# A written order for VectorE's first steps, one query load on another queue, and block sums moved later

## The chip, the cores and the metric

The program runs on one core of one Trainium2 chip. The metric is the device time of one execution in microseconds (us), as the median of several runs. A core has five engines with queues of their own: TensorE (PE, matmuls), VectorE (DVE), ScalarE (ACT), GpSimd (POOL) and SyncE (SP, which here only issues DMAs). An engine takes its instructions strictly in the order of its queue; an instruction that waits holds up everything behind it on the same engine.

## The reference

An attention with a local window and block summaries, then two gated layers over its output, in fp32:

```python
# q, k, v: (2, 8, 768, 64); block 32, window 16, nb = 24
k_sum = k.reshape(B, H, nb, block, D).max(axis=3)
v_sum = v.reshape(B, H, nb, block, D).mean(axis=3)
scores_l = where(|pos_q - pos_k| < window, scale * q @ k^T, -1e9)
scores_s = scale * q @ k_sum^T + log(block)
a = softmax over concat([scores_l, scores_s])      # + 1e-9 in the denominator
attn = a @ concat([v, v_sum])
x = attn as (1536 tokens, 512)
h = x @ w_in;  x = (h * sigmoid(1.702 * h)) @ w_out          # d_ff 2048
y = (sigmoid(x @ w_gate) * (x @ w_val)) @ w_out2             # d_ff 1536
```

The layers' weights arrive as 64-bit floats.

## The kernel before

**Units.** The attention is cut into 24 units: 2 batches, 3 groups of 256 tokens (`g`), 4 pairs of heads (`hp`). Unit u is (batch, g, hp) with hp fastest, so units 0 to 11 are batch 0. For each unit the kernel runs, in this order:

- `w_copy` (POOL): scales the keys of the group and the block maxima of the keys (`kmax`, from `prep_k` on VectorE, one per batch and pair of heads) into a tile `kx`, of which there are two.
- `b_pe` (TensorE): scores `ps_s` from `kx` and the unit's queries (`load_q`), on top of a mask.
- `b_max` (VectorE): the row maximum `nm`. `b_exp` (ScalarE): four exponentials with row sums. `n_inv` (VectorE): adds epsilon to the sums and takes the reciprocal `rr`. `n_mul` (POOL): multiplies.
- `c_pe` (TensorE): transposes; `c_copy` copies them out (ScalarE for the first ten units, then VectorE).
- `d_pe` (TensorE): products with a window `vwin`, whose rows are the values of the group (`load_v`) and the block sums of the values (`put_v`, a DMA from the tile `vsum`). For the first group of batch 0 the sums come by separate matmuls straight from `vsum`. `d_hi` and `d_lo` write the result as two parts, `xH` and `xL`.

**Block sums of the values.** `sum_load` loads one pair of heads, transposed, through SP (batch 1 through two buffers, so the third load waits for the first sum). `sum_v` reduces it on VectorE into `vm`, and `sum_lay` lays the four out with matmuls on TensorE (`ps_v`) and scales them on ScalarE into `vsum`. `put_v` then copies `vsum` into a window.

**The loop.** One Python loop runs t from -1 to 26. In iteration t the parts stand as `ORDER` says: `w_copy` of unit t+1, scores, maximum and exponentials of unit t, reciprocal of t-1, multiplication of t-2, transposes and products of t-3. The products of unit 0 come one iteration later, behind `sum_lay(0)` at t = 4. The loads, sums and weight steps of the iteration stand behind them. `pull` runs the next step of the weight decode (`load`, lines 106 to 167: `da`, `db`, hi and lo parts of a weight, on VectorE and ScalarE; a step may issue the next weight DMA through `fetch`). `next(fill)` adds matmuls of the first layer for tokens already done (`filler`; ps_h into the hidden, ps_o out of it); the steps for the first 512 tokens begin at t = 10.

**Who sets the order.** SP's queue keeps the order of the source (`manual_schedule`). On the other engines a planner at compile time places the instructions by its own estimate of time, with the source's order as priority. `behind(a, b)` forbids it to place a ahead of b; it adds no wait on the chip. Before the change it holds for POOL (`in_turn`, to unit 8), for TensorE's scores among themselves, for `sum_lay(0)` behind the newest scores, and for batch 0's sums behind the newest maximum. VectorE's other steps have no written order.

**After the attention** the two layers run on TensorE from a written order of products; it is not touched.

Of the kernel before, what the change touches and what calls it, by code (L numbers as in the profile page):

```python
# [24 lines left out]
EPS = 1e-9  # L25
# [4 lines left out]
def attention_moe_moe2_kernel(ctx: ExitStack, tc: tile.TileContext, ins: dict, out: bass.AP):  # L30
# [544 lines left out]
    IN_TURN = 8  # L575
    coming = (x for n, key in enumerate(wanted) for x in load(*key, n < 2))
# [13 lines left out]
    with tc.manual_schedule(engines={mybir.EngineType.SP}), ExitStack() as es:  # L590
# [15 lines left out]
        SH = S + 2 * HALO  # L606

# [44 lines left out]
        def sum_v(b, hp):  # L652
# [7 lines left out]
            if b == 0:  # L660
                behind(ins, topped[-1])

        def sum_lay(b):
            r = vpart.pop(b)
            ps = ps_a.tile([W0, H * D], F32, tag="x", name="ps_v", bufs=2)
            for hp in range(HP):
                ins = nc.tensor.matmul(ps[:, hp * P:(hp + 1) * P], lhsT=r[:, hp], rhs=ident, start=True, stop=True)
                if b == 0:
                    behind(ins, scored[-1])
            nc.scalar.activation(vsum[b][0:W0], ps, AF.Copy, scale=1.0 / BLK)  # L670

        def prep_k(b, hp):
# [3 lines left out]
            nc.vector.tensor_reduce(out=ks[:, 0:NB], in_=own, axis=AX.X, op=ALU.max)  # L676
# [12 lines left out]

        live, scored, topped, spread = {}, [], [], []  # L690

        def behind(a, b):

            tc.add_manual_dep(
                a.ins, b.ins.name,
                mybir.DependencyInfo(mybir.DependencyClass.NoSync, mybir.DependencyReason.DATA), reason="order",
            )

        def in_turn(ins, u):

            if u <= IN_TURN:
                if spread:
                    behind(ins, spread[-1])
                spread.append(ins)
# [13 lines left out]
        def b_max(u):  # L718
            nm = sp.tile([P, G], F32, tag="nm", name="nm")
            topped.append(nc.vector.tensor_reduce(out=nm, in_=live["s", u], axis=AX.X, op=ALU.max, negate=True))  # L720
# [12 lines left out]
        def n_inv(u):  # L733
            rs = sp.tile([P, G], F32, tag="rs", name="rs")
            nc.vector.tensor_scalar(out=rs, in0=live.pop(("sum", u)), scalar1=EPS, scalar2=None, op0=ALU.add)
            rr = sp.tile([P, G], F32, tag="rr", name="rr")
            nc.vector.reciprocal(out=rr, in_=rs)
# [69 lines left out]
        for i in range(HP):  # L807
            load_q(i, nc.scalar)
            load_k(0, i)
        for i in range(HP):  # L810
            sum_load(0, i)
        load_v(0, 0)
        load_q(4, nc.sync)
        load_q(5, nc.sync)
        load_v(0, 1)
        load_q(6, nc.sync)
        load_q(7, nc.sync)
        fetch()
# [37 lines left out]
        for t in range(-1, NU + LD):  # L856
# [3 lines left out]
            if u < NU and units[u][1] == 0:  # L860
                prep_k(units[u][0], units[u][2])
            for part, lag in ORDER:
# [3 lines left out]
                if 0 <= t - lag < NU and not (late and t == LD):  # L866
                    part(t - lag)
                if (part, t) == (b_pe, LD + 1):
# [4 lines left out]
            if 0 <= t < HP:  # L873
                sum_v(0, t)
# [4 lines left out]
            if t in (7, 8, 9, 10):  # L879
                sum_load(1, t - 7)  # L880
            if t in (8, 9, 10, 11):
                sum_v(1, t - 8)
# [164 lines left out]
```

## Time and profile before

| | us |
|---|---|
| runs | 620.97, 621.0, 622.27 (median 621.0) |
| profiled execution, its own time | 620.25 |
| span, first to last instruction | 618.5 |
| TensorE busy in the span | 602.6 (97%) |
| VectorE | 465.8 (75%) |
| ScalarE | 307.6 (50%) |
| POOL | 213.5 (35%) |

The span of the profiled execution is 1.75 us shorter than its time; what lies around it is launch and end. The profile has several views. Busy time by stretch shows which engine is full where. An engine's order of time gives each instruction with its start, its length and, in brackets, the idle time before it and what ended that. The list of waits sums these up. The chain that ended last is followed back from the last instruction. DMAs are listed with the time from issue to landing. In all of them `out<-in` names the tiles and L12 is a line of the kernel. Two records of one matmul (x8 for four) stand where an fp32 matmul runs in two passes. Tile names carry no unit number: units are counted from the first.

### The profile page before, as it was taken

To read this page: it belongs to the slowest core of one execution; us is meant where nothing else is said; L and a number is where in the kernel's file an instruction comes from. 1 tells how busy PE (TensorE), PEld (TensorE's weight loads), DVE (VectorE), ACT (ScalarE), POOL (GpSimd) and SP (SyncE) were. 2 spreads that over 40 slices of the span, in tenths; PEclk is the share of its full clock that TensorE was granted. 3 is DMA by queue.
4 is the path that set the end of the run, shared out by engine and by line. 5 is a ranking of instruction groups with operands and counts; after the bars stand their busy time and mean duration, and the time that the engine had idled before them with its cause. 6 is when DMAs were issued, how large, how long until landed. Compare 5 with 4: busy or idle time off the path is not lost.

```text
span 618.5 us, 8840 instructions
## 1 busy us (share of the span) xinstructions
PE 602.6 (97%) x3356; PEld 500.6 (81%) x3360; DVE 465.8 (75%) x684; ACT 307.6 (50%) x614; POOL 213.5 (35%) x168
## 2 busy tenths in 40 slices
PE   7898999999999999999999999999999999999997
PEld 3775778788878888888888898888898898898896
DVE  7499665389998778796769889576968768877434
ACT  5587757656443354434445566644335435444230
POOL 6897686323372413232241232021121121131030
PEclk9799999999999999999999999999999999999999
DMA  9999733035121103040102013310312222100014
GB/s 325 333 305 340 239 86 69 2 103 170 68 69 68 40 30 137 1 137 3 67 0 69 1 29 110 134 69 27 110 69 69 68 69 70 68 1 1 0 48 156
DMA packets 25162, 58.10 MB, mean 94 GB/s; under 512 B 1569, under 2 KB 1825, under 8 KB 25121
## 3 DMA queue, kind: packets, MB, share of 16 engines
q1 hardware_dynamic: 24400, 56.24, 27.8%
q10 hardware_dynamic: 720, 1.31, 0.6%
q8 instruction: 26, 0.43, 0.3%
q14 instruction: 16, 0.12, 0.1%
HBM read 53.08 MB, written 3.15 MB: 91 GB/s over the span
## 4 chain that ended last, share of the span: by engine, by line
PE 80%; issue 5%; DVE 5%; DMA 4%; ACT 3%; POOL 3%; SPq 0%; ACTq 0%; POOLq 0%; DVEq 0%
PE ps_o L474 33%; PE ps_y L178 15%; PE ps_x L178 10%; PE ps_v L178 10%; PE ps_h L474 4%; PE ps_h L178 4%; DMA q<-in_q 2%; POOL gl L494 2%; PE ps_x L767 2%; PE ps_s L714 2%; DMA raw<-in_moe_w_out 1%; PE ps_p L748 1%; ACT e L728 1%; DVE db L123 1%; DVE sg L485 1%
## 5 line engine op out<-in xcount | busy, mean ns | idle before, releaser
L494 POOL TENSOR_TENSOR gl<-sg,gh 128x512 fp32r<-128x512 f32 x84 | 126.0, 1506 | 361.7 <-ACT gh L493 259.8
L557 DVE TENSOR_TENSOR acc<-ps_o,acc 128x512 f32<-128x512 f32 x143 | 96.0, 683 | 46.7 <-PE ps_o L474 46.6
L493 ACT CAST gh<-sg 128x512 fp32r<-128x512 f32 x84 | 51.5, 620 | 49.4 <-DVE sg L485 39.9
L474 PE MATMUL ps_o<-gl,w_1H 128*128 128x512 f32 x192 | 75.5, 394 | 0.5 <-POOL gl L494 0.5
L474 PE MATMUL ps_o<-gh,w_1H 128*128 128x512 f32 x192 | 74.7, 390 | 0.0
L474 PE MATMUL ps_o<-gh,w_1L 128*128 128x512 f32 x192 | 72.5, 397 | 1.0 <-ACT acc L553 0.9
L474 PE MATMUL ps_o<-w_2L,gh 128*128 128x512 f32 (+1 forms) x146 | 56.7, 388 | 0.0
L474 PE MATMUL ps_o<-w_2H,gh 128*128 128x512 f32 (+1 forms) x146 | 56.3, 387 | 0.0
L474 PE MATMUL ps_o<-w_2H,gl 128*128 128x512 f32 (+1 forms) x146 | 56.2, 389 | 0.1
L137 DVE SCALAR_TENSOR_TENSOR da<-da,db 128x1024 uint32<-128x1024 uint32 x34 | 47.7, 1402 | 5.6 <-ACT da L131 4.8
L131 ACT ACTIVATE da<-da 128x1024 f32<-128x1024 f32 x34 | 36.1, 1061 | 23.5 <-DVE da L123 23.4
L474 PEld LDWEIGHTS ps_o<-gh,w_1L 128*128 128x128 f32 x192 | 36.0, 188 | 9.0 <-ACT acc L553 1.4
L474 PEld LDWEIGHTS ps_o<-gl,w_1H 128*128 128x128 f32 x192 | 36.1, 188 | 8.6 <-POOL gl L494 1.5
L474 PEld LDWEIGHTS ps_o<-gh,w_1H 128*128 128x128 f32 x192 | 36.1, 188 | 7.2
L728 ACT ACTIVATE e<-ps_s,nm 128x128 f32<-128x128 f32 x96 | 34.2, 377 | 8.1 <-DVE nm L720 5.9
L474 PE MATMUL ps_h<-xL,w_0H 128*128 128x512 f32 x96 | 37.9, 395 | 0.2 <-DVE xL L788 0.2
L474 PE MATMUL ps_h<-xH,w_0L 128*128 128x512 f32 x96 | 37.8, 402 | 0.3 <-ACT xH L785 0.3
L474 PE MATMUL ps_h<-xH,w_0H 128*128 128x512 f32 x96 | 37.5, 390 | 0.0
L687 POOL TENSOR_SCALAR kx<-k 128x384 f32<-128x384 f32 x24 | 32.0, 1334 | 14.0 <-PE ps_s L714 8.7
L485 DVE TENSOR_TENSOR sg<-ps_h,sg 128x512 f32<-128x512 f32 x32 | 21.8, 682 | 14.2 <-ACT sg L501 12.1
L474 PEld LDWEIGHTS ps_o<-w_2H,gh 128*128 128x128 f32 x146 | 27.4, 188 | 5.7
L714 PE MATMUL ps_s<-kx,q 128*128 128x128 f32 x192 | 27.7, 287 | 4.3 <-DMA q<-in_q 2.1
(242 smaller groups left out, 1502.8 us busy)
## 6 DMA issues: line engine op xcount, KB each, us to landing
raw<-in_moe_w_out SPq DMA_DIRECT2D x13, 1024.0 KB, 4.9
raw<-in_moe_w_in SPq DMA_DIRECT2D x8, 1024.0 KB, 7.3
raw<-in_moe_w_gate SPq DMA_DIRECT2D x6, 1024.0 KB, 5.1
raw<-in_moe_w_val SPq DMA_DIRECT2D x6, 1024.0 KB, 5.1
q<-in_q SPq DMA_DIRECT2D x20, 256.0 KB, 9.7
vwin<-in_v SPq DMA_DIRECT2D x6, 768.0 KB, 9.4
k<-in_k SPq DMA_DIRECT2D x8, 400.0 KB, 6.8
out<-acc SPq DMA_DIRECT2D x11, 256.0 KB, 2.0
```

The source lines that it names most:

```text
L131: nc.scalar.activation(af, af, AF.Prelu, scale=REBIAS, alpha=-2.0 ** 32)
L137: nc.vector.scalar_tensor_tensor(out=a, in0=a, scalar=3, in1=b, op0=ALU.logical_shift_left, op1=ALU.bitwise_or)
L178: nc.tensor.matmul(ps, lhsT=a[x][:, kk, :], rhs=b[y][:, kk, :], start=start and i == 0, stop=i == n - 1, skip_group_check=True,)
L474: nc.tensor.matmul(ps, lhsT=a, rhs=b, start=i == 0, stop=i == n - 1)
L485: nc.vector.tensor_tensor(out=sg, in0=val, in1=sg, op=ALU.mult)
L493: nc.scalar.copy(gh, sg)
L494: nc.gpsimd.tensor_tensor(out=gl, in0=sg, in1=gh, op=ALU.subtract)
L557: nc.vector.tensor_tensor(out=a[:, m, :], in0=ps, in1=a[:, m, :], op=ALU.add)
L687: in_turn(nc.gpsimd.tensor_scalar(out=to, in0=x, scalar1=scale, scalar2=None, op0=ALU.mult), u)
L714: ins = nc.tensor.matmul(ps[:, j, :], lhsT=t[:, j, :], rhs=kt[:, j, :], start=False, stop=j == G - 1)
L728: nc.scalar.activation(e[:, j, :], s[:, j, :], AF.Exp, bias=nm[:, j:j + 1], accum_out=sm[:, j:j + 1])
L767: nc.tensor.matmul(ps[64 * e:64 * e + 64, j, :], lhsT=x[:, h * D:(h + 1) * D], rhs=y[:, j, 64 * e:64 * e + 64], start=n == 0, stop=n == le ...
```

## The change

Four parts, all in the attention and its loop.

1. A chain `next_up` on VectorE: each instruction handed to it is placed behind the one before. In it stand batch 0's key maxima and value sums, the row maxima and the two reciprocal steps of units 0 to 4, the row maxima from unit 10 on and batch 1's value sums. `prep_k` moves from the head of the iteration to behind `b_max`; batch 0's sums move to the places below.
2. The queries of unit 4 (`load_q(HP, nc.scalar)`) are issued by ScalarE's queue, ahead of the sums' loads in the source; those of unit 5 go ahead of the first value window, those of units 6 and 7 ahead of the second.
3. Batch 1's value-sum loads move from t = 7 to 10 to t = 8 to 11, the sums from t = 8 to 11 to t = 10 to 13, `sum_lay(1)` from t = 11 to t = 13.
4. `sum_lay(1)` is now behind the newest scores too, and the copy `put_v(1, 0)` follows it at t = 13 instead of standing at t = 11.

```diff
+    FIRST_UNITS = 5
...
+        def next_up(ins, when=True):
+            if when:
+                if turn:
+                    behind(ins, turn[-1])
+                turn.append(ins)
...            # sum_v
-            if b == 0:
-                behind(ins, topped[-1])
+            next_up(ins)
...            # sum_lay
-                if b == 0:
-                    behind(ins, scored[-1])
+                behind(ins, scored[-1])
...            # prep_k
-            nc.vector.tensor_reduce(out=ks[:, 0:NB], in_=own, axis=AX.X, op=ALU.max)
+            ins = nc.vector.tensor_reduce(out=ks[:, 0:NB], in_=own, axis=AX.X, op=ALU.max)
+            if b == 0:
+                next_up(ins)
...            # b_max
-            topped.append(nc.vector.tensor_reduce(out=nm, in_=live["s", u], axis=AX.X, op=ALU.max, negate=True))
+            ins = nc.vector.tensor_reduce(out=nm, in_=live["s", u], axis=AX.X, op=ALU.max, negate=True)
+            next_up(ins, u < FIRST_UNITS or u >= NU // 2 - 2)
...            # n_inv, both of its instructions
+            next_up(ins, u < FIRST_UNITS)
...            # loads ahead of the loop
+        load_q(HP, nc.scalar)
         for i in range(HP):
             sum_load(0, i)
+        load_q(5, nc.sync)
         load_v(0, 0)
-        load_q(4, nc.sync)
-        load_q(5, nc.sync)
-        load_v(0, 1)
         load_q(6, nc.sync)
         load_q(7, nc.sync)
+        load_v(0, 1)
...            # the loop
-            if u < NU and units[u][1] == 0:
-                prep_k(units[u][0], units[u][2])
             for part, lag in ORDER:
...
+                if part is b_max and u < NU and units[u][1] == 0:
+                    prep_k(units[u][0], units[u][2])
+                if part is b_max and t in (2, 3):
+                    sum_v(0, t - 1)
...
-            if 0 <= t < HP:
-                sum_v(0, t)
+            if t in (1, 3):
+                sum_v(0, 0 if t == 1 else 3)
...
-            if t in (7, 8, 9, 10):
-                sum_load(1, t - 7)
             if t in (8, 9, 10, 11):
-                sum_v(1, t - 8)
-            if t == 11:
+                sum_load(1, t - 8)
+            if t in (10, 11, 12, 13):
+                sum_v(1, t - 10)
+            if t == 13:
                 sum_lay(1)
+                put_v(1, 0)
...            # at t = 7, 11, 15, 19
                 load_v(c // NG, c % NG)
-                put_v(c // NG, c % NG)
+                if c != NG:
+                    put_v(c // NG, c % NG)
```

## Rows read from the trace of the kernel before

**Rows 1.** Stretch: length; busy PE, PEld, DVE, ACT, POOL; clock; DMA share; GB/s

```profile
0.00:15.40 15.40, 10.85 (x51) 5.86 (x51) 11.42 (x35) 8.21 (x27) 10.36 (x18) 1.00 0.91 325
15.40:22.30 6.90, 4.49 (x20) 3.61 (x21) 2.38 (x7) 2.58 (x10) 6.90 (x9) 0.51 1.06 300
25.00:50.00 25.00, 23.69 (x285) 18.84 (x284) 23.23 (x46) 21.86 (x81) 20.83 (x17) 1.00 1.05 329
50.00:70.00 20.00, 16.88 (x125) 12.37 (x127) 18.75 (x29) 16.44 (x43) 13.80 (x11) 1.00 0.80 252
100.00:600.00 500.00, 499.50 (x2538) 421.31 (x2538) 384.31 (x519) 238.62 (x391) 136.03 (x88) 1.00 0.17 59
```

**Rows 2.** TensorE in order of time: start, us, what [idle before <-releaser]

```profile
14.85 0.66 PE L748 MATMUL ps_p<-ident,e 128*128 128x128 f32 x4 [1.75 <-POOL e L742]
17.58 2.04 PE L714 MATMUL ps_s<-kx,q 128*128 128x128 f32 x8 [2.08 <-DMA q<-in_q]
19.56 1.92 PE L667 MATMUL ps_v<-ident,vm 128*32 128x128 f32 x8
...
23.88 1.16 PE L714 MATMUL ps_s<-kx,q 128*128 128x128 f32 x8
```

**Rows 3.** The chain that ended last, in order: start, us, what

```profile
8.63 8.82 DMA q<-in_q
...
61.94 1.51 ACT e L728 x8
...
114.01 5.49 PE ps_h L474 x24
```

**Rows 4.** VectorE in order of time, 8 to 16 us

```profile
8.80 0.68 DVE L720 TENSOR_REDUCE nm<-ps_s 128x4 f32<-128x512 f32 x1
...
11.05 0.94 DVE L656 TENSOR_REDUCE vm<-vt 128x24 f32<-128x768 f32 x1
...
13.44 0.17 DVE L737 RECIPROCAL rr<-rs 128x4 f32<-128x4 f32 x1
...
15.10 0.94 DVE L656 TENSOR_REDUCE vm<-vt_early 128x24 f32<-128x768 f32 x1
```

**Rows 5.** POOL in order of time, 13 to 26 us

```profile
13.76 1.04 POOL L742 TENSOR_TENSOR e<-e,rr 128x512 f32<-128x512 f32 x1 [2.43 <-DVE rs L735]
...
16.39 1.04 POOL L742 TENSOR_TENSOR e<-e,rr 128x512 f32<-128x512 f32 x1
...
25.20 1.17 POOL L687 TENSOR_SCALAR kx<-k 128x384 f32<-128x384 f32 x1 [2.50 <-PE ps_s L714]
```

**Rows 6.** DMAs issued in 6.9-8, 36.1-36.5, 38.1-39, 52.5-52.8: count, KB, us to landing

```profile
vt_early<-in_vt SPq DMA_DIRECT2D x1, 384.0 KB, 6.8
...
raw<-in_moe_w_out SPq DMA_DIRECT2D x1, 1024.0 KB, 13.3
...
k<-in_k SPq DMA_DIRECT2D x1, 400.0 KB, 13.2
...
vt<-in_vt SPq DMA_DIRECT2D x1, 384.0 KB, 6.3
```

**Rows 7.** VectorE in order of time, 42 to 75 us

```profile
42.30 0.94 DVE L656 TENSOR_REDUCE vm<-vt 128x24 f32<-128x768 f32 x1
...
46.02 0.68 DVE L720 TENSOR_REDUCE nm<-ps_s 128x4 f32<-128x512 f32 x1
...
49.67 0.68 DVE L123 TENSOR_SCALAR db<-raw 128x1024 uint32<-128x1024 uint32 x1
...
74.42 1.26 DVE L123 TENSOR_SCALAR db<-raw 128x1024 uint32<-128x1024 uint32 x1 [2.33 <-DMA raw<-in_moe_w_out]
```

**Rows 8.** TensorE's waits, 50 to 70 us: us in total, times, longest

```profile
PE ps_v L667 <- DVE vm L656: 1.2, 3, 0.7
...
PE ps_s L714 <- POOL kx L687: 0.8, 1, 0.8
```

**Rows 9.** SP's waits 40 to 80 us, and its order of time

```profile
SPq L635 <- ACT xH L785: 10.7, 1, 10.7
...
64.88 0.61 SPq L635 DMA_DIRECT2D vwin<-vs  x1
```

More of the change, by code (lines that the diff above doesn't have):

```diff
@@ L606, in attention_moe_moe2_kernel, with behind, in_turn @@
         SH = S + 2 * HALO
+        live, scored, spread, turn = {}, [], [], []
+        def behind(a, b):
+            tc.add_manual_dep(
+                a.ins, b.ins.name,
+                mybir.DependencyInfo(mybir.DependencyClass.NoSync, mybir.DependencyReason.DATA), reason="order",
+            )
+        def in_turn(ins, u):
+            if u <= IN_TURN:
+                if spread:
+                    behind(ins, spread[-1])
+                spread.append(ins)
+        def next_up(ins, when=True):
[3 more added lines that the diff above has]
+                turn.append(ins)
         def load_k(b, hp):
@@ L688, in w_copy @@
             kx[u] = t
[L690 to L704, printed above, removed]
         def b_pe(u):
@@ L734, in n_inv @@
             rs = sp.tile([P, G], F32, tag="rs", name="rs")
-            nc.vector.tensor_scalar(out=rs, in0=live.pop(("sum", u)), scalar1=EPS, scalar2=None, op0=ALU.add)
+            ins = nc.vector.tensor_scalar(out=rs, in0=live.pop(("sum", u)), scalar1=EPS, scalar2=None, op0=ALU.add)
+            next_up(ins, u < FIRST_UNITS)
             rr = sp.tile([P, G], F32, tag="rr", name="rr")
-            nc.vector.reciprocal(out=rr, in_=rs)
+            ins = nc.vector.reciprocal(out=rr, in_=rs)
+            next_up(ins, u < FIRST_UNITS)
             live["rr", u] = rr
```

## The prediction

> **What bounds the kernel now.** I read the busy time of each engine by stretch first [rows 1]. From 100 to 600 us TensorE is busy 499.5 of 500 us at the full clock, so what is won or lost ahead of 100 us comes out at the end one for one, unless another engine becomes later than TensorE there. What is left to win lies ahead: 4.55 us idle to 15.4, 2.41 us to 22.3, 1.31 us from 25 to 50, 3.12 us from 50 to 70. In the second stretch the granted clock is 0.51, the lower of the two levels (1.2 GHz), so its work takes twice as long as well.
>
> Second, TensorE's own order of time says what it stood before [rows 2]. Ahead of unit 0's transposes (14.85) it waits 1.75 us for POOL, after them 2.08 us for unit 4's queries. Unit 4's scores then take 2.04 us where unit 5's, at the full clock, take 1.16, and the block sums laid out behind them take 1.92, about 1.0 at the full clock (half). Only then come the first products with the values and unit 5's scores at 23.88. Third, the chain of waits gives the reason for the longer wait [rows 3]: the queries of unit 4 are issued at 8.63 and are 8.82 us under way, to 17.45. Fourth, VectorE's and POOL's order [rows 4, 5]: VectorE reduces block sums (0.94 each) between unit 0's maximum at 8.80 and its reciprocal at 13.44. POOL, which takes each unit's kx and each multiplication in a fixed order, stands idle 2.43 us for that reciprocal, and later 2.50 us for unit 5's scores. Last, the transfers. From 15 to 50 us the DMA share is 1.05 to 1.06 [rows 1]: there, data land in the order of their bytes, however soon the engines are done.
>
> **The change part by part.** No instruction is added or removed. Work per engine stays as it is, one DMA issue goes from SP to ScalarE, and the rest is order. So the sum is one of waits, made in the profiled execution: span 618.5, time 620.25, the 1.75 us around it unchanged. The median of the runs shown is 621.0, 0.75 above; that is added at the end.
>
> *VectorE's order to unit 4, and unit 4's queries.* Each step is dated anew from the rows.
> - Unit 0's maximum runs at 8.80 for 0.68 us, its exponentials take 1.51 [rows 3], so its sum is there at about 11.0 even if the maximum comes no sooner (it now stands ahead of the third key maximum and may). The reciprocal, now ahead of all block sums, follows at about 11.3, not 13.44.
> - POOL has been free since 13.76 - 2.43 = 11.33, so unit 0's multiplication starts there: 2.4 us sooner. One round of POOL, multiplication and next kx, is 16.39 - 13.76 = 2.63 us [rows 5], so unit 4's kx is done at about 14.0, unit 5's at 16.6.
> - Unit 4's queries now go out behind the first loads and ahead of most of the value sums' inputs. They land between 9 (right behind 2.69 MB of keys and queries, 8.3 us at the 325 GB/s of the stretch) and 14.6 (behind the sums' inputs), about when unit 4's kx is there or before. ScalarE has nothing but two fills ahead of the first maximum (9.48), which cover the issue; without cover it costs ScalarE one issue, 0.61 us by SP's largest row [rows 9]. Price: 256 KB more ahead of the sums' inputs, 0.8 us; the last (issued near 7, 6.8 under way [rows 6]) lands at 13.8 + 0.8 = 14.6.
> - The sums now stand in VectorE's queue among the maxima, behind the reciprocal: at about 11.4, 12.9, 14.6 and 16.0. The last was at 15.10 [rows 4], so it is 0.9 later and done at 16.9. It is what is late next, no longer the queries nor kx (14.0).
> - Unit 4's scores run at 14.1 to 15.3, the lay-out of the sums from 16.9 to 17.9, ScalarE's scaling to 18.5. The first value window stands behind two query tiles where unit 4's queries stood behind it and none: 17.45 + 0.8 = 18.3. So the first products start at 18.5, and unit 5's scores at about 19.7 instead of 23.88: 4.2 us, if the clock stays up.
>
> *The clock.* It is at 0.51 in the stretch that holds the queries' wait, shortly after POOL's [rows 1, 2]. The new order leaves one wait of about 1.6 us, for the last sum. Bounds: no stretch at the lower level, gain 4.2; the same stretch, with the lay-out, the first products and the scores at double time, about 2.2 us given back, gain 2.0. I take the first: the longer wait goes.
>
> The Trainium skill, "TensorE: Matmul & The Clock Gate", Part 1, says that the throttled state is the default and activity releases it; that speaks for the lower bound wherever a wait stays. The trace agrees as far as it goes (0.51 around the waits, 1.00 once the engine is dense), and by that rule alone the gain would be the 2.0 above.
>
> A rule against moving the queries to ScalarE is in "DMA: Bandwidth & Descriptors" of the Trainium skill, section Issuing engines are not separate DMA queues: another issuing engine saves issue time only. The trace agrees (share 1.06, nothing left to hand out); by it 4.2 us come from the place in the order alone, and the 0.8 us that others pay stand in full.
>
> *The middle, 25 to 50.* VectorE is busy 23.2 of 25 us beside the full DMA share. The second group's output weight lands at about 49.5 (issued near 36.2, 13.3 under way), the second batch's first keys at 51.4 (38.2 and 13.2) [rows 6]. VectorE takes the weight up at 49.67 [rows 7], 0.2 after it landed, and TensorE waits 0.8 us for the keys' kx [rows 8]. One of the sums' inputs of 384 KB stood ahead of each of the two and now stands behind it: 384 KB at 329 GB/s is 1.2 us. So at 50 to 54 us two ends meet: the engines are 4.2 us ahead, the data 1.2. In the 3.0 us between, TensorE has only filler, 24 matmuls of 5.5 us a step [rows 3], if VectorE and ScalarE have its gate ready. Bounds: all bridged, 0 lost; nothing, 3.0 lost. Nearest row: VectorE only 0.2 us behind the data speaks for 3.0, while the gate itself needs no late data. I take the middle, 1.5 lost.
>
> *The second batch's sums, 50 to 70.* Loads one iteration later, sums two, lay-out behind unit 13's scores. What goes: TensorE's three waits for single sums, 1.2 us [rows 8], and part of a block on SP. The copy of the sums into the value window holds SP's queue for 10.7 us, to 64.88 [rows 9], with the last keys, queries and two weight loads behind it; now the last keys and two query loads pass ahead of it. What is added: unit 11's maximum (46.02) stands behind the first sum (42.30) in VectorE's queue [rows 7], and this sum's input now lands behind the weight of 49.5, at about 49.4 with the order moved. Unit 11's exponentials and transposes wait for it, 4 us longer than now; behind the sum on VectorE stand gates and decode steps, and TensorE waits for those. The next unit needs keys of 50 us anyway. Further inputs wait for a buffer, that is for the sum two before, and took 6.3 us under way [rows 6]: sums at 50, 53, 57 and 60, lay-out at 61. So the copy leaves SP at about 62, 3 us sooner, and the weight behind it, for which VectorE stands 2.33 us at 74.42 [rows 7], lands sooner too. Bounds for TensorE's 3.12 us of idle: all gone, or as much new waiting as goes (worse is a rival). I take 0.5 us gained, the 1.2 of the three waits less one new one of 0.7, their longest.
>
> Sum: 4.2 - 1.5 + 0.5 = 3.2 us. 620.25 - 3.2 = 617.05, with 0.75 for the median 617.8.
>
> **The rivals.**
> - *All of it passes.* The filler bridges the middle and half of the 3.1 us goes: 4.2 + 1.6 = 5.8, so 615.2. For it: 5.5 us of filler a step. Against: VectorE's 0.2 us at 49.67.
> - *Data swallow it.* VectorE, in a fixed order, stands before data at 50, or the clock falls as before; between 0 and 1.2 us stays: 620.4 in the middle. For it: the share of 1.05.
> - *The second sums are held back, and it gets slower.* In a full queue transfers took 13 us, not 6.3 [rows 6]. If the last input, issued near 53, does, it lands at 66, its sum is done at 67 and the copy leaves at 68.6, 3.7 us after 64.88. The weight of 74.4 then lands at 78, and the gates behind it on VectorE stop TensorE by about 3.5 us. With data holding the front's gain at 1.2: 621.0 + 2.3 = 623.3. It decides once the last input lands after about 62. Against it: the queue is less full then (share 0.80 from 50 to 70).
> - *It does not do what it says.* What stands outside the written order is placed anew at compile time; if decode steps slip in among the maxima, the front stays as it is: 621.0, give or take 0.5.
>
> **How the numbers follow.** Forecast (616.0 to 619.4) 0.55; all passes 0.16; swallowed 0.13; slower 0.10; no effect 0.06. A measurement here tells about 0.2% from none, 1.24 us. Faster: 0.55 + 0.16 + a third of the swallowed case, 0.05 with rounding, 0.76. Slower: 0.10, and 0.01 of no effect. Same: the rest, 0.13. The range runs from 614.6, just past the case in which all passes, to 621.6, which leaves out most of the slower case.
>
> **What would show it.** Right: no wait for queries among TensorE's, unit 0's multiplication on POOL before 12, unit 5's scores near 20, the clock at 1.00 there; SP's wait ahead of the copy well under 10.7 us; TensorE's idle time from 50 to 70 under 3. Wrong: a wait of VectorE for a sum's input of some us near 12 or 50, the lay-out at a clock of 0.5, a copy that leaves SP after 65. The prediction fails as a whole if TensorE is idle anew between 100 and 600.

## The result, and the profile after

The changed kernel takes 626.12 us (median of 4 runs, 625.18 to 626.61) where the kernel before takes 621.08 in the same job. The ratio is 1.0075 [1.0057, 1.0092]: slower by 5.0 us, where 3.2 us of gain were forecast. The profiled execution has a span of 624.2 us.

The same stretches as in [rows 1], of the kernel after:

```profile
0.00:15.40 15.40, 11.30 (x59) 6.84 (x59) 11.55 (x34) 8.91 (x30) 12.23 (x20) 1.00 0.91 332
15.40:22.30 6.90, 5.68 (x82) 4.46 (x83) 4.34 (x11) 3.75 (x18) 6.90 (x9) 1.00 1.07 270
25.00:50.00 25.00, 18.27 (x190) 15.18 (x191) 16.88 (x35) 17.17 (x58) 13.56 (x13) 0.86 1.02 328
50.00:70.00 20.00, 15.74 (x125) 11.26 (x125) 18.31 (x29) 15.47 (x42) 12.57 (x10) 0.91 0.75 241
100.00:600.00 500.00, 499.02 (x2548) 419.86 (x2544) 383.19 (x518) 241.49 (x400) 137.68 (x91) 1.00 0.18 60
```

To 22 us the forecast came true: TensorE does more, and the clock that was 0.51 is 1.00. Then the gain is lost more than once over: 25 to 50 us has 5.4 us less of TensorE's work, part of it at the lower level, and 50 to 70 us another 1.1 us less. From 100 to 600 us TensorE stands only 0.5 us more than before.

The front in detail, TensorE's order of time (against [rows 2]):

```profile
14.44 1.16 PE L722 MATMUL ps_s<-kx,q 128*128 128x128 f32 x8 [0.83 <-POOL kx L711]
...
17.23 0.41 PE L690 MATMUL ps_v<-ident,vm 128*32 128x128 f32 x2
...
18.75 0.33 PE L778 MATMUL ps_x<-pt,vwin 128*64 128x64 f32 x2 [1.11 <-DMA vwin<-in_v]
...
19.01 1.16 PE L722 MATMUL ps_s<-kx,q 128*128 128x128 f32 x8
...
22.77 1.16 PE L722 MATMUL ps_s<-kx,q 128*128 128x128 f32 x8
...
30.28 1.09 PE L759 MATMUL ps_p<-ident,e 128*128 128x128 f32 x4 [6.14 <-issue]
```

Unit 4's scores run at 14.44 (17.58 before), unit 5's at 19.01 (23.88). Then, at 30.28, TensorE has stood 6.14 us. The reason is in ScalarE's order of time, where `ACTq` is a DMA issue:

```profile
18.59 0.57 ACT L692 ACTIVATE vs<-ps_v 32x512 f32<-32x512 f32 x1
...
27.07 0.73 ACTq L659 DMA_DIRECT2D vwin<-vs  x1
27.92 0.37 ACT L737 ACTIVATE e<-ps_s,nm 128x128 f32<-128x128 f32 x1 [8.07 <-DMA raw<-in_moe_w_in]
...
29.56 0.62 ACT L764 COPY pt<-ps_p 128x512 f32<-128x512 f32 x1
```

The sums are scaled at 18.59, and the copy of them into the second value window (`put_v(0, 1)`, which the kernel before too sends on ScalarE's queue) goes out at 27.07. Everything behind it on ScalarE waits, the next exponentials (8.07 us, put down to the landing of the first weight) and the copy of the transposes at 29.56, at whose end TensorE goes on. That weight was issued at 12.58 and 14.4 us under way, to 26.98:

```profile
raw<-in_moe_w_in SPq DMA_DIRECT2D x1, 1024.0 KB, 14.4
```

Counted in the order of the issues, the first weight is the eighth before the copy. In the kernel before, where one query load less stands ahead of the copy, the eighth was unit 7's queries (issued at 11.6, 11.2 us under way, so landed at about 22.7), and the copy left right behind them:

```profile
22.81 0.72 ACTq L635 DMA_DIRECT2D vwin<-vs  x1
```

That in this program an issue waits for the landing of the transfer eight issues before it is read from these two orders and from two further kernels below.

SP's waits from 50 to 85 us, and the issue of its copy of the second batch's sums (compare [rows 9]):

```profile
SPq L659 <- ACT xH L796: 10.0, 1, 10.0
SPq L673 <- DVE vm L680: 9.0, 2, 6.5
```
```profile
79.02 0.60 SPq L659 DMA_DIRECT2D vwin<-vs  x1
```

It left at 64.88 before. A table for all that follows: per stretch, TensorE's idle time (length less busy) and, as an estimate, what the clock took (busy times one less the granted clock), in us, from the busy time by stretch of each run. The differences between its sums follow those between the spans to within 2.4 us. To 25 us seven kernels with the front of the kernel before give 9.2 to 10.9, so a difference of a us in one place says little. The last four of these kernels lack or move the first copy, as told below.

```
                       0-25    25-50   50-70  70-130   median
before                 9.6      1.3     3.1     0.8    621.0
after                  6.2      9.0     5.7     0.5    626.1
second half alone      9.2      1.7     6.9     1.3    623.4
front, copy on ACT     5.4      9.0     3.7     1.3    624.7
front, copy on SP      7.2      3.0     6.0     1.1    621.3
front, no copy         6.5      4.1     2.3     0.6    619.4
change, no copy        5.0      4.8     2.5     1.1    620.2
before, no copy        9.2      0.9     2.0     4.1    623.5
```

### The profile page after: what moved, and what is told of

It is laid out like the page before. It is cut to its first block, busy times and chain, and to the rows that moved or that the text cites. A ratio compares the mean times of both kernels' runs of the same rounds, so it can differ in the third digit from the quotient of the medians.

```text
span 624.2 us, 8837 instructions
## 1 busy us (share of the span) xinstructions
PE 602.8 (97%) x3360; PEld 501.6 (80%) x3360; DVE 464.3 (74%) x684; ACT 308.5 (49%) x614; POOL 210.9 (34%) x168
## 4 chain that ended last, share of the span: by engine, by line
PE 82%; issue 6%; ACT 4%; POOL 3%; DMA 3%; DVE 2%; ACTq 0%; POOLq 0%; DVEq 0%
PE ps_o L474 33%; PE ps_y L178 15%; PE ps_x L178 10%; PE ps_v L178 10%; PE ps_h L474 5%; PE ps_h L178 3%; PE ps_s L722 2%; PE ps_x L778 2%; POOL gl L494 2%; PE ps_p L759 1%; DMA vwin<-in_v 1%; DMA q<-in_q 1%; ACT e L737 1%; ACT da L131 1%; POOL t1L L258 1%
## 5 line engine op out<-in xcount | busy, mean ns | idle before, releaser
L137 DVE SCALAR_TENSOR_TENSOR da<-da,db 128x1024 uint32<-128x1024 uint32 x34 | 45.2, 1329 | 6.6 <-ACT da L131 6.1
L131 ACT ACTIVATE da<-da 128x1024 f32<-128x1024 f32 x34 | 36.1, 1063 | 24.3 <-DVE da L123 22.4
L474 PEld LDWEIGHTS ps_o<-gh,w_1L 128*128 128x128 f32 x192 | 36.1, 189 | 10.5 <-ACT gh L493 2.9
L737 ACT ACTIVATE e<-ps_s,nm 128x128 f32<-128x128 f32 x96 | 34.2, 375 | 15.2 <-DMA raw<-in_moe_w_in 8.1
L711 POOL TENSOR_SCALAR kx<-k 128x384 f32<-128x384 f32 x24 | 30.2, 1259 | 12.7 <-PE ps_s L722 11.3
L485 DVE TENSOR_TENSOR sg<-ps_h,sg 128x512 f32<-128x512 f32 x32 | 21.7, 682 | 14.4 <-ACT sg L501 12.3
L753 POOL TENSOR_TENSOR e<-e,rr 128x512 f32<-128x512 f32 x24 | 26.4, 1104 | 16.6 <-DVE rr L747 14.1
```

What stands on the lines that cost most here:

```text
L131: nc.scalar.activation(af, af, AF.Prelu, scale=REBIAS, alpha=-2.0 ** 32)
L137: nc.vector.scalar_tensor_tensor(out=a, in0=a, scalar=3, in1=b, op0=ALU.logical_shift_left, op1=ALU.bitwise_or)
L474: nc.tensor.matmul(ps, lhsT=a, rhs=b, start=i == 0, stop=i == n - 1)
L485: nc.vector.tensor_tensor(out=sg, in0=val, in1=sg, op=ALU.mult)
L711: in_turn(nc.gpsimd.tensor_scalar(out=to, in0=x, scalar1=scale, scalar2=None, op0=ALU.mult), u)
L737: nc.scalar.activation(e[:, j, :], s[:, j, :], AF.Exp, bias=nm[:, j:j + 1], accum_out=sm[:, j:j + 1])
```

## The experiments

**The copy's queue, and the two halves.** First the change with one word less, the copy on SP's queue; then the front half alone, and the second half alone:

```diff
-                    put_v(0, 1, nc.scalar)
+                    put_v(0, 1)
```


> The changed kernel with one edit: the copy of the first batch's sums into the second window goes out on SP's queue instead of ScalarE's. Theory A (ScalarE's queue stands 8 us behind that copy, which itself waits for the landing of the first layer's first weight): ScalarE's wait of 8.07 us goes, unit 5's exponentials end by 21, TensorE's idle time from 25 to 50 us falls from 6.7 to under 2.5, and the time from 626.1 to 617 to 620. Rival B (the loss comes from the second batch's later sums): the wait goes, but the time stays at 624 or above. Rival C (data swallow the front): 620 to 622, with VectorE waiting for weights near 27 and 50 in ScalarE's place.

```diff
 # the change without: next_up for unit 10 on, sum_load/sum_v/sum_lay of batch 1 later, put_v(1, 0) later
```


> The change without its second half: VectorE's written order to unit 4 and the new places of the query loads stay, the second batch's loads, sums, lay-out and copy are as before the change. The copy of the first sums is still on ScalarE's queue, behind the same weight. Theory A: ScalarE still stands some 8 us, time 624 to 627. Rival B: the loss goes with the second half, 616 to 619.

```diff
 # the kernel before, with only these
-            if t in (7, 8, 9, 10):
-                sum_load(1, t - 7)
+            if t in (8, 9, 10, 11):
+                sum_load(1, t - 8)
+            if t in (10, 11, 12, 13):
+                sum_v(1, t - 10)
...
```


> The kernel before with only the second half of the change: the second batch's loads one iteration later, the sums two, the row maxima from unit 10 on and these sums in a written order, lay-out and copy at t = 13. Theory A: the front is as before, so 620 to 622.5. Rival B: slower by most of the loss, 624 to 627, with the copy leaving SP near 75 or later instead of 64.9.

Measured (the ratio to the kernel before of the same job in brackets, here and below): copy on SP 625.29 (1.0074 [1.0059, 1.0089]), front half 624.70 (1.0065 [1.005, 1.008]), second half 623.38 (1.0041 [1.0027, 1.0055]). So each half loses. The front half loses with the same wait of ScalarE (8.0 us). In the first run that wait is gone and units 5 to 8 run 4 to 5 us sooner than before, but nothing of it is left at unit 9 (35.68, before 35.71), and from 50 to 60 us TensorE then stands 5.3 us (1.8 before). So in the whole change the copy's other queue alone gives back only 0.8 us. The second half lies between the ranges of both its theories.

Whether such a wait alone does it was tried in the kernel before, where the first weight's load was put one place ahead:

```diff
-        load_q(7, nc.sync)
         fetch()
+        load_q(7, nc.sync)
```


> The kernel before with two neighbours in SP's queue swapped: the first layer's first weight is loaded ahead of unit 7's queries. By the order of the waits the copy of the first sums on ScalarE's queue then waits for that weight (landing near 25) and not for unit 7's queries (22.7). Theory A: ScalarE stands some 2 us longer, the next unit's scores and all behind them come as much later, 622 to 624. Without theory A: 620.5 to 621.5, or a little faster since the weight lands 0.8 us sooner.

Measured: 625.17, 1.0073 [1.0058, 1.0088]. ScalarE's order of time there:

```profile
24.84 0.72 ACTq L635 DMA_DIRECT2D vwin<-vs  x1
25.61 0.58 ACT L753 COPY pt<-ps_p 128x512 f32<-128x512 f32 x1 [3.82 <-DMA raw<-in_moe_w_in]
```

So with no step of the change, the swap makes the copy wait for the first weight, as its theory A had it, and costs 4.2 us, more than the 1 to 3 us of that theory. The copy leaves 2.0 us later than before. By the same estimate as in the table, TensorE loses 1.5 us more than before from 25 to 50 us and 4.7 us more from 50 to 130, and gains 1.8 to 25. So the wait is shown; that it alone makes all of the 4.2 us is not.

**The front half without that wait.** The copy on SP; then also the first weight ahead of the second value window; then VectorE's first decode step behind unit 7's maximum:

```diff
-                    put_v(0, 1, nc.scalar)
+                    put_v(0, 1)
```


> The front half of the change alone (VectorE's order of the first units and unit 4's queries early), the second half as before, and the copy of the first block sums into the value window goes out on SP's queue instead of ScalarE's. Theory A: the change had two faults, the copy that stops ScalarE for 8.1 us and the chain of the second sums, and each alone gives back the whole front gain; without both the front's lead of 4 to 5 us at unit 8 (28.2 instead of 33.5) is mostly swallowed by the landing of the first weight near 26.7, since VectorE stands before it: 619 to 622, unit 9 near 35.7 as in the kernel before. Theory B: the front gain survives once both faults are gone: 616 to 618, unit 11 some 3 us sooner than 43.4. Theory C: the front itself makes the middle worse: over 623.

```diff
-        load_v(0, 1)
         fetch()
+        load_v(0, 1)
```


> As the run with the front half alone and the copy on SP, but the first weight (1 MB) is asked for ahead of the second value window instead of behind it. Theory A (VectorE stands before the first weight, in a fixed order, with row maxima behind it): the weight lands some 1 to 2.5 us sooner, VectorE's wait of 2.9 us for it shrinks by as much, units 7 to 9 come sooner, and the time falls by 1 to 2 us against that run. Theory B (the data as a whole are the limit from 15 to 50 us, or the later value window costs the products of units 4 to 7 as much): within 0.7 us of that run. Theory C: the lead is given back at the next weights (26 to 50 us) whatever the first one does: the wait moves to a later decode step, within 0.7 us.

```diff
+            if (layer, g, i) == (1, 0, 0) and maxima:
+                tc.add_manual_dep(
+                    ins.ins, maxima[-1].ins.name,
...            # that is behind(ins, maxima[-1]); and pull() from t = 7 on
```


> As the run with the front half alone and the copy on SP, but VectorE's first decode step of the first weight is placed behind the row maximum of unit 7, and the decode steps are handed out from iteration 7 on, as many by iteration 9. Bytes and their order stay. Theory A (what gives the lead back is the row maxima queued behind the wait for the weight): no wait of VectorE for the first weight over 1 us with a maximum behind it, units 7 to 9 at 25.3, 28.2 and about 31 to 33 instead of 35.7, time 1 to 3 us below that run. Theory B (the lead is limited by the later data: second weight, keys of the second batch at 50 us): the units of the first batch come sooner, but TensorE waits near 50 to 60 us and the time is within 0.7 us of that run.

Measured: copy on SP 621.30 (1.0001 [0.9991, 1.001]), weight ahead of the window 626.55 (1.0095 [1.0062, 1.0128]), decode later 626.49 (1.0092 [1.0067, 1.0117]). The first is as its theory A had it: ScalarE's wait cost the front half 3.4 us, and without it neither gain nor loss is left. The other two were misses of all their theories, which had the time as it was or 1 to 3 us better. VectorE's wait for the weight was not all that holds unit 9. The copy and the first products of unit 4, which need it, in the second of these runs (SP's order, its time to landing, TensorE's order):

```profile
19.57 0.74 SPq L659 DMA_DIRECT2D vwin<-vs  x1
```
```profile
vwin<-vs SPq DMA_DIRECT2D x1, 256.0 KB, 14.6
```
```profile
34.22 1.12 PE L780 MATMUL ps_x<-pt,vwin 128*64 128x64 f32 x16 [3.26 <-DVE da L137]
```

19.57 + 14.6 = 34.2: TensorE starts when the copy lands (the step named as releaser, a decode step that these products do not read, ended at 33.67). In the other two runs it lands at 35.6 and 35.8, and the products begin at 35.74 and 35.86, after waits of 0.35 and 2.51 us. The two slower kernels lose their further 5 us later, at 70 to 100 us above all (idle 2.8 and 4.1); by which step was not followed.

Order alone, and queries alone:

```diff
 # VectorE's written order as in the change; load_q(4) stays on SP behind load_v(0, 0)
```


> Of the change only VectorE's order of the first five units; unit 4's queries stay on SP behind the first value window, the second half as before, the copy stays on ScalarE's queue. Theory A: the copy waits on ScalarE for an earlier transfer that is not the first weight here (its turn is the one of unit 7's queries, landed near 22.7), so ScalarE isn't stopped; unit 0's multiplication comes 2 us sooner on POOL, but unit 4's scores still wait for the queries at about 17.4, as before: 620 to 621.5. Theory B: the order alone gives most of the front's gain: 617 to 619.5. Theory C: the new order itself, not the copy, makes the loss: over 623.

```diff
+        load_q(HP, nc.scalar)                # loads as in the change; VectorE's order as before
```


> Of the change only unit 4's queries by ScalarE's queue, with the reordered loads; VectorE's order and the second half as before, the copy of the first sums on ScalarE's queue. It waits for unit 7's queries there, which have landed by 21 to 23, so ScalarE isn't stopped. Theory A (two causes hold unit 4 in the kernel before, the late queries and POOL's wait for unit 0's reciprocal): without the wait for queries unit 4's scores come 1 to 2 us sooner, but the copy's landing holds the products of unit 4 near 34: 619.5 to 621.5. Theory B: the queries alone bring the front's whole gain: 617 to 619.

Measured: order alone 621.08 (0.9999 [0.999, 1.0009]), queries alone 625.02 (1.0056 [1.0038, 1.0074]). The first is as its theory A had it: unit 4 waits 4.92 us for its queries, at 18.51. The second was a miss of both theories. Unit 4 came at 14.98, but the new order of the loads put the second value window eight issues ahead of the copy, and ScalarE stood 4.83 us:

```profile
23.91 0.73 ACTq L635 DMA_DIRECT2D vwin<-vs  x1
24.68 0.37 ACT L728 ACTIVATE e<-ps_s,nm 128x128 f32<-128x128 f32 x1 [4.83 <-DMA vwin<-in_v]
```

So the copy on ScalarE's queue was kept, but one issue earlier; and then taken away, with the sums read from their own tile:

```diff
+            if copied:                       # in load_q: the next query load
+                behind(ins, copied.pop())    # stands behind the copy
```


> The front half alone, with the copy of the first block sums on ScalarE's queue, but issued ahead of unit 12's query load in the order of issue, so that it waits for an earlier transfer that has landed (unit 7's queries) and not for the first weight; the second half as before. Theory A: what takes the front's lead back is the landing of this copy, which the first products through the second value window need. On SP's queue it was 13.8 to 14.7 us under way and landed at 34.2 to 35.9, and these products began within 0.1 us of it in three runs; on ScalarE's queue the copies took 7.2 to 8.4. So: issue near 19.5 to 20, landing near 28, no wait of ScalarE over 1 us near 20, those products at 29 to 32 instead of 35.1, unit 9's scores 2 us or more sooner than 35.7, time 616.5 to 619.5. Theory B: the middle is limited by the weights and keys whatever the copy does: TensorE's waits move to a weight or to the keys near 50 us, 620.5 to 622. Theory C: ScalarE still waits for the first weight (as in the change): 624 to 626.

```diff
-                    if (b, g) == (0, 0):
+                    if b == 0 and g < 2:     # matmuls from vsum for units 4 to 7 too
...
-                    put_v(0, 1, nc.scalar)
```


> The front half alone, without the copy of the first block sums into the second value window: units 4 to 7 read the sums from their own tile in matmuls of their own, as units 0 to 3 do (8 more small matmuls per product, 32 in all for each of four units, about 0.5 us a unit on TensorE), and the first fill of the value windows is twice as long on ScalarE. No wait on ScalarE and no landing of a copy is left in the way. Theory A (the copy is what takes the front's lead back): the products of unit 4 begin at 28 to 30 instead of 35.1, time 617 to 620, of which 2 us are paid for the added matmuls where TensorE isn't idle. Theory B (weights and keys limit the middle): 620.5 to 623.5.

Measured: copy one issue earlier 621.24 (1.0001 [0.9991, 1.0011]), no copy 619.44 (0.9979 [0.9968, 0.999]). In the first the copy left at 21.74 and landed 8.1 us later, at 29.8, early enough; still nothing was won, and the first products of unit 4 ran at 36.50 instead of 29 to 32. What stood in its place, in VectorE's order:

```profile
28.49 1.37 DVE L123 TENSOR_SCALAR da<-raw 128x1024 f32<-128x1024 f32 x1 [2.24 <-DMA raw<-in_moe_w_in]
```

Theory A fell there: the copy's landing is one bound, and the first weight, with maxima behind it, reads as another. In all eight kernels that have the new front and no long wait of ScalarE, unit 9's scores stand at 34.4 to 36.5 us (35.71 before), copy or no copy. No run takes both bounds away. Without the copy the front half is faster than the kernel before.

**The second half's loss.** Unit 11's maximum freed from the first sum; four buffers for the value tiles; the second copy on POOL's queue, with the second half and without it:

```diff
-            next_up(topped[-1], u >= NU // 2 - 2)
+            next_up(topped[-1], u >= NU // 2)
```


> The kernel before with the second half of the change only, but the chain of VectorE's order for the second batch begins at unit 12: unit 11's row maximum doesn't stand behind the first of the second sums. Theory A (the second half loses because unit 11's exponentials come behind the first sum, so behind the sigmoids and a change of ScalarE's table, and the gates wait behind them): unit 11's exponentials near 48 as in the kernel before, TensorE busy 50 to 60 near 8 instead of 6.2, time 620.5 to 622.2 instead of 623.4. Theory B (the second half loses by its late loads and the copy that leaves SP at 72 instead of 65): 622.8 to 624.5.

```diff
-                t = vp.tile([P, S], F32, tag="vt", bufs=2, name=f"vt{b}_{hp}")
+                t = vp.tile([P, S], F32, tag="vt", bufs=4, name=f"vt{b}_{hp}")
```


> The kernel before with the second half of the change only, and four buffers instead of two for the second batch's value tiles, so that the third and fourth load don't wait on SP's queue for the sums of the first and second (6.8 us of SP's waits with two buffers), and nothing behind them does. Theory A (the loss of the second half is SP's queue held by those waits, which makes the third and fourth sums late: 61.7 and 67.4 instead of 56.1 and 60.7): third load leaves by 48, sums by 62, the copy leaves SP near 66, time 620.5 to 621.7. Theory B (the loss is the place of the sums in VectorE's order and of the lay-out behind unit 13's scores; the copy still leaves SP at 70 or later): 622.5 to 624.

```diff
-                put_v(1, 0)
+                put_v(1, 0, nc.gpsimd)
```


> The kernel before with the second half of the change only, but the copy of the second batch's sums goes out on POOL's queue, so that SP's queue isn't held for it and the weight loads behind it leave without it. Theory A (the loss is what stands behind the late copy on SP: the weights left at 72.7 and 74.3 instead of 67.5 and 68.5): these weights leave before 66, TensorE busy from 70 to 100 near 30, and the time falls to 619.5 to 621.5. Theory B (the loss is at 50 to 60, where TensorE was busy 6.2 instead of 8.2 us, whatever the copy does): 622.5 to 624.

> The kernel before, with only the copy of the second batch's sums on POOL's queue instead of SP's, where it stood 10.7 us with the last keys, queries and two weight loads behind it. Theory A (that wait is hidden, since the weight of 74.4 costs TensorE nothing by 100): 620.3 to 621.7. Theory B (SP's wait costs): the keys and weights leave near 55 to 58, VectorE's wait of 2.33 us at 74.42 goes, 618.5 to 620. Theory C (POOL stands before the copy, with kx of unit 15 behind it): 622 to 624.

Measured: maximum freed 624.21 (1.0051 [1.0036, 1.0066]), four buffers 622.93 (1.0033 [1.002, 1.0046]), copy on POOL 623.22 (1.0036 [1.0023, 1.0049]), the kernel before with the copy on POOL 623.68 (1.0049 [1.0032, 1.0065]); the second half as it is had 623.38. None of the three cures it. VectorE's sums and SP's copy of the second half alone:

```profile
52.09 0.94 DVE L665 TENSOR_REDUCE vm<-vt 128x24 f32<-128x768 f32 x1
...
56.75 0.93 DVE L665 TENSOR_REDUCE vm<-vt 128x24 f32<-128x768 f32 x1
...
61.74 0.94 DVE L665 TENSOR_REDUCE vm<-vt 128x24 f32<-128x768 f32 x1
...
67.45 0.94 DVE L665 TENSOR_REDUCE vm<-vt 128x24 f32<-128x768 f32 x1
```
```profile
72.03 0.60 SPq L644 DMA_DIRECT2D vwin<-vs  x1
```

Before, they stand at 42.30, 51.62, 56.06 and 60.67. With four buffers the third load leaves at 49.15 instead of 53.06, and the sums stay where they are (57.36, 62.99, 68.41). With the copy on POOL the weight behind it leaves at 65.84 instead of 72.68. The stretch of 50 to 70 us is nearly the same in these two as in the second half alone, busy time by stretch (second half alone, four buffers, copy on POOL):

```profile
50.00:70.00 20.00, 15.84 (x115) 12.69 (x116) 19.45 (x31) 16.34 (x42) 13.48 (x12) 0.83 0.76 248
```
```profile
50.00:70.00 20.00, 15.58 (x113) 12.52 (x115) 19.82 (x30) 15.46 (x40) 12.65 (x11) 0.83 0.79 251
```
```profile
50.00:70.00 20.00, 15.41 (x112) 12.58 (x113) 19.42 (x31) 15.24 (x41) 13.72 (x12) 0.83 0.84 270
```

So neither the buffers nor SP's queue make the loss. TensorE waits in all three for `pt` (1.9 us near 54) and for `gh` (1.6 to 2.3 near 58), and the granted clock of the stretch is 0.83 (1.00 before). In the second half alone:

```profile
54.56 0.84 PE L778 MATMUL ps_x<-pt,vwin 128*64 128x64 f32 x16 [1.88 <-ACT pt L764]
...
58.16 1.22 PE L474 MATMUL ps_o<-gh,w_1L 128*128 128x512 f32 x2 [1.71 <-ACT gh L493]
```

Both are results of ScalarE. Unit 11's maximum stands behind the first sum there, and its exponentials come 8 us later than before, behind the gates' sigmoids and with a load of ScalarE's table ahead of them (VectorE's order, then ScalarE's):

```profile
52.96 0.68 DVE L730 TENSOR_REDUCE nm<-ps_s 128x4 f32<-128x512 f32 x1
```
```profile
54.53 1.28 ACT L739 ACT_TABLE_LOAD   x1
55.83 0.37 ACT L739 ACTIVATE e<-ps_s,nm 128x128 f32<-128x128 f32 x1
```

In the kernel before, ahead of the sigmoids:

```profile
47.88 0.38 ACT L728 ACTIVATE e<-ps_s,nm 128x128 f32<-128x128 f32 x1
```

But this is not the whole cause: with the maximum freed these exponentials run at 51.27, ahead of the sigmoids, and TensorE waits 3.29 us for `pt` at 55.99 instead. Which step of ScalarE's order makes the loss is open.

The kernel before with the copy on POOL shows how a gain is given back. The first weight behind the copy leaves at 63.50 (67.53 before), and 70 to 100 us is full; then, from 100 to 130:

```profile
70.00:100.00 30.00, 30.00 (x236) 24.65 (x236) 19.04 (x42) 17.65 (x62) 22.81 (x25) 1.00 0.45 113
100.00:130.00 30.00, 26.67 (x221) 20.22 (x221) 13.20 (x30) 20.14 (x55) 9.24 (x8) 1.00 0.01 2
```

The kernel before has 29.20 and 29.97 there. From 100 to 130 us TensorE now waits 2.2 us for `gh` and 0.8 for `gl`; that the last units have less other work left beside them is a guess, and not shown.

**Do the parts add up?** The front without the first copy and the second copy on POOL; the whole change without the first copy; the kernel before without it:

```diff
+                put_v(c // NG, c % NG, nc.gpsimd if c == NG else nc.sync)
```


> The front half without the copy of the first sums (units 4 to 7 read the sums from their own tile; this alone measured 619.4), and the copy of the second batch's sums on POOL's queue. Theory A: the two are independent; with SP free from 56 on the keys of unit 15 (VectorE waited 3.7 us for them at 71.2) and the weights come sooner, 617 to 619. Theory B: SP's wait is hidden: 619 to 620.2. Theory C: POOL stands before the copy: over 621.

```diff
 # the whole change, and in it as above: if b == 0 and g < 2, no put_v(0, 1)
```


> The whole change, with the copy of the first sums taken away: units 4 to 7 read the sums from their own tile. Theory A (the parts add up: the front half without the copy measured 619.4, the second half alone cost 2.4 us): 621 to 622.6. Theory B (the second half costs more the earlier the first batch is done, as with the copy on SP's queue, where it took 4.0 us): 622.8 to 624.5.

```diff
 # the kernel before, and in it the same
```


> The kernel before, without the copy of the first sums: units 4 to 7 read them from their own tile (about 2 us of added matmuls), nothing of the change. Theory A (the gain of the front half without the copy, 1.5 us, is the front half's, kept once the copy's landing is out of the way): here 620.5 to 622.8. Theory B (the gain is that of the missing copy alone, and the front half gives nothing): 618.8 to 620.

Measured: front without the copy and POOL 621.61 (1.0013 [1.0004, 1.0023]), change without the copy 620.15 (0.9991 [0.9981, 1.0]), the kernel before without it 623.53 (1.0038 [1.0023, 1.0053]). The first is as its theory C had it: the second copy on POOL costs 2 to 3 us here as in the kernel before. The other two miss their ranges, one on the fast side of both, one on the slow side of both; the parts do not simply add up. They do settle the copy's part: taking it away gives the changed kernel 5.2 us by the ratios (6.0 by the medians of two jobs) and costs the kernel before 2.6. They settle less what the change is worth without it: 623.53 - 620.15 = 3.4 us against the like kernel, and 0.8, hardly clear of noise, against the kernel before, which has no added matmuls. The stretch of 25 to 50 us, in the changed kernel without the copy and in the kernel before without it:

```profile
25.00:50.00 25.00, 21.52 (x275) 18.08 (x270) 20.09 (x38) 18.01 (x59) 15.21 (x14) 0.93 1.05 342
```
```profile
25.00:50.00 25.00, 24.15 (x332) 20.20 (x332) 23.02 (x45) 20.50 (x71) 21.49 (x18) 1.00 1.05 334
```

What the front gains to 25 us (4.2 in the table) is nearly all given back here (3.9), in TensorE's waits for `e` and `pt` at 31 to 33 us. The net comes from 70 to 130 us, where the kernel before without the copy loses 4.1 us and the changed one 1.1. Why it does was not tried.

## Why the prediction was wrong, step by step

- **VectorE's order to unit 4, and unit 4's queries: right.** Forecast and measured: reciprocal 11.3 and 11.31, unit 4's scores 14.1 and 14.44, last of the lay-out from 16.9 and at 17.23, first products 18.5 and 18.75, unit 5's scores 19.7 and 19.01. 4.2 us were forecast; unit 5 came 4.9 sooner.
- **The clock: right to 25 us.** No stretch there is at the lower level, and the 0.83 and 1.11 us of waits that stay did not bring it down. It falls behind the wait of 6.14 us, which the forecast did not have. The bound was real, though: in the front half with the copy on SP the wait for the first value window was 1.87 us instead of 1.11, the granted clock from 20 to 25 us 0.66, and unit 8 came at 31.25 instead of 28.22 (the change with the copy on SP, clock 1.00). It also differs between executions of one kernel: in the front half without the copy three of ten have a mean granted clock of 1.000 (618.2 to 619.1 us) and two of 0.994 (620.6 and 621.4, of which the second is the profiled one).
- **The step that failed: "ScalarE has nothing but two fills ahead of the first maximum (9.48), which cover the issue".** It looked at the query load that was moved, and at what stood ahead of it on ScalarE; it gave a price of 0.61 us. It did not ask which later issue the new order of loads would hold. The copy of the first sums stands on ScalarE's queue behind their scaling, and its issue waits for another transfer, that of eight issues before. The change put the first weight there. ScalarE stands 8.07 us; before, the copy left 0.7 us behind the end of the scaling. The front half alone was to gain 2.7 us (4.2 - 1.5) and loses 3.7 (624.70 against 620.99). Taken away in two ways, by SP's queue (621.30) and by one place in the order (621.24), the wait gives 3.4 of these 6.4 us back; the other 3.0 are the next point. The trace of before could have shown it: the copy left at 22.81, 0.1 behind the landing of unit 7's queries.
- **"The middle, 25 to 50": mis-sized.** 1.5 us were to be lost; with the copy out of the way it is 3.2 to 3.9 (table: 0.9 without the change, 4.1 and 4.8 with it). In the front half with the copy on SP it is 1.7, but 2.9 more go from 50 to 70 us (3.0 and 6.0 against 1.3 and 3.1). The bound meant was at 50 us; the ones seen are at 28 (first weight) and 34 to 36 (the copy, where it goes by SP).
- **"The second batch's sums": wrong in sign.** 0.5 us gained was forecast; alone the second half costs 2.4 us, and on top of the front half with the copy on SP 4.0. (On top of the front half with the copy on ScalarE it costs 1.4 and without the copy 0.7, which is not clear of noise.) The term that failed is "less one new one of 0.7": unit 11's exponentials were to come 4 us later and came 8 us later, and two new waits of 1.88 and 1.71 us stand where one was priced. The sums were forecast at 50, 53, 57 and 60 and the copy at 62. In the changed kernel they run at 54.92, 58.77, 65.15 and 69.44 and the copy leaves at 79.02. They do not stand where their inputs land: the last was there by about 63 (in the second half alone by about 61, its sum at 67.45), and four buffers, which bring the inputs sooner, did not move them.
- **The rivals.** "Data swallow it" (620.4) is near what came in the front half alone where ScalarE was free and the copy was kept, 621.3 and 621.2; the whole change with the copy on SP had 625.3. "The second sums are held back" had its event, a copy that leaves after 68.6, and its sign; its place was wrong, for with the weight behind the copy sooner (65.84) the loss stays. Its point of decision, an input that lands after about 62, was just passed in the changed kernel (59.73 + 3.5 = 63.2), but not by a slow transfer: the load had waited for its buffer. "All of it passes" was not seen, and "It does not do what it says" is excluded by the first rows. Of the signs of being wrong one came, the copy that leaves SP after 65.

The kernel with the front half alone and no first copy, 619.44 us, is faster than both kernels, by 0.21% [0.10, 0.32] against the kernel before. How much of that is the order and how much the clock of its executions is not separated.

## What to carry to other kernels

When the order of DMAs is changed, go through every issue on a computing engine's queue, not only at those that move: each may wait for the landing of an older transfer, and all work behind it stands. Read from the trace of before what each such issue left behind, and count whether the same transfer still stands there. A lead of 4 us at the front is worth what the next landings let through; date those (first weight, first copy) before the gain is booked.

## What the runs showed that was not expected

The first copy (256 KB) was 13.8 to 14.7 us under way in four kernels where it went by SP's full queue (issued at 19.6 to 21.8), and 7.2 to 8.5 us in twelve where it went by ScalarE's (21.7 to 27.1), at about the same DMA share of 1.05. In the kernel before, the copy's queue then has 17.8% of the engines' time beside 84.9% of SP's, from 25 to 30 us. The prediction drew on the section Issuing engines are not separate DMA queues of the Trainium skill's "DMA: Bandwidth & Descriptors", by which another issuing engine saves issue time only; for the time of one transfer that doesn't hold here. Another section of that page, Queues, rings and completion order, says that each DMA engine goes round between the queues a packet at a time. The measured times agree with it so far that the transfer on the emptier queue overtakes what was issued before it on the full one; why its share was 17.8% and not nearer to half is not shown. So the prediction's reading that data land in the order of their bytes does not hold across two queues.

At a full share the rate differs. In the kernel before it was 227 GB/s from 40 to 45 us and 396 from 50 to 55, at shares of 1.06 and 1.04. So a full share doesn't say when bytes land.
